# Plain PSUM copies of K and Q, zero-plane K, fixed V slots and paired 64x64 projections in a two-layer attention and token-MLP kernel

## The chip, the cores and the metric

The kernel runs on one core of a Trainium2 chip. The core has five engines with a queue of instructions each: TensorE (PE; its weight loads are listed apart as PEld), VectorE (DVE), ScalarE (ACT), GpSimd (POOL) and SyncE (SP, which here only issues DMAs). Each engine works through its own queue in order and waits on semaphores where an instruction needs the result of another engine. The metric is the device time of one execution in microseconds, lower is better. Where a number has no unit below, it is microseconds.

## What is computed

Two attention blocks and two token-mixing MLPs in turn on an activation of 2048 tokens by 512 channels, in bf16. Attention has 32 heads of 16 channels and a causal window of 256 tokens; the MLP mixes along the tokens, with 1792 hidden units.

```python
def _A_ref(x, wqkv, wo):
    B, S, D = x.shape                      # 1, 2048, 512
    H = 32; Dh = D // H; W = 256
    qkv = (x @ wqkv).reshape(B, S, 3, H, Dh).transpose(2, 0, 3, 1, 4)
    q, k, v = qkv[0], qkv[1], qkv[2]
    scores = jnp.einsum("bhqd,bhkd->bhqk", q, k) * (Dh ** -0.5)
    idx = jnp.arange(S)
    mask = (idx[:, None] - idx[None, :] >= 0) & (idx[:, None] - idx[None, :] < W)
    p = _softmax(jnp.where(mask[None, None], scores, -1e9), axis=-1)
    o = jnp.einsum("bhqk,bhkd->bhqd", p, v)
    return o.transpose(0, 2, 1, 3).reshape(B, S, D) @ wo

def _B_ref(x, w1, b1, w2, b2):
    h = _layernorm(x, axis=-1)
    u = _gelu(jnp.einsum("bsd,sf->bdf", h, w1) + b1)
    y = jnp.einsum("bdf,fs->bds", u, w2) + b2
    return y.transpose(0, 2, 1)

x = x + _A_ref(_layernorm(x), A_wqkv, A_wo)
x = x + _B_ref(_layernorm(x), B_w1, B_b1, B_w2, B_b2)
x = x + _A_ref(_layernorm(x), A_wqkv, A_wo)
x = x + _B_ref(_layernorm(x), B_w1, B_b1, B_w2, B_b2)
```

## The kernel before

**Tiling of attention.** The tokens are taken in four spans Q of 512. In each span the 512 channels are four tiles t of 128, eight heads each. For each (Q, t) there are nine steps m: step m lets each block of 32 queries meet one block of 32 keys of the window, so nine steps cover the 256 keys before a query and its own block. `bank_segments` gives the two or three stretches of queries in a step that use one key block each, and `emit_scores` (L688) makes four matmuls per stretch, in the four 64x64 quarters of the array. A quarter works on 64 channels (four heads) and yields two heads by 32 keys, so the other heads' channels must be zeroed on one side. A step is then `emit_scores` into two of the PSUM banks 0 to 3, one exp over both banks on ScalarE (`emit_exp`, L699), a multiplication of the edge of the window (L716, VectorE or GpSimd), and `emit_pv` (L737), which multiplies with V in 64x64 quarters too and accumulates in banks 4 and 5. There are 144 steps in a layer. When the ninth step is done, the two banks are copied out (`copy_out`, L360 or L362), sums of the softmax go by DMA to `den_c`, their reciprocal is spread by 64x64 matmuls (L781) and multiplied in (L788).

**Masks.** `project` (L530) makes a tile of K, Q or V: four matmuls of 128x128 by 512 tokens into bank 6 or 7. `masked` (L541 on VectorE, L546 on ScalarE) takes K and Q out of PSUM twice as wide as they are: each value times a column that is one or zero, so that K has two copies with half the heads zeroed and Q two with even or odd 16-channel groups zeroed. `job_v` copies a V tile (L360, L362), transposes it in 32x32 blocks on VectorE (L605) and spreads it beside a static pattern of ones (L590), which yields the sums of the softmax.

**The rest.** `job_outproj` (L657) multiplies by wo, adds the residual (L661) and takes statistics (L464). LayerNorm is `ln_stats` and `ln_apply`. `job_transpose` brings a normalised tile to channel-major form, by TensorE (L519) in the first span of a layer and by DMA (L511) in the others. `u_product` (L864) is the first MLP product, `job_u_part` part of it ahead of time, during the last two spans of attention; `job_u` adds the gelu (L912). `job_y` (L937) is the second product, 16 tiles of tokens; in layer 0, eight of these come before the attention of layer 1 starts and eight are put among it. Weights w1 and w2 are loaded into whatever buffers are free then (`w1_place`, `w2_place`): `w1buf`, `xhT`, `k_sb`, `q_sb`, `oU`.

**What sets the order.** Each operation is registered with `plan.op`, with the tiles that it reads and writes, and gets a number in the order of registration. `ORDER` holds, for each engine, the queue as a list of these numbers, two characters each; it is fixed in the file, and `Plan.needs` derives the semaphore waits from the dependences. The durations given to `plan.op` don't act on the order any more, only on the order of several waits of one instruction. `BANKS` says for each projection whether it goes to bank 6 or 7. SP's queue has all loads and stores, DMA transposes and the moves from `oU` and `o2`, in order.

Of the kernel before, what the change touches and what calls it, by code (L numbers as in the profile page):

```python
# [6 lines left out]
dt = mybir.dt  # L7
ALU = mybir.AluOpType
# [6 lines left out]
WARM = 10  # L15
NPARTS = (6, 6)
PARTQ = (0, 1)
UP0, UPD = 0.5, 3.3
MASKED = 1215
# [10 lines left out]
ArAsAtAuAvBGBIAwAxBKBMBQBOBUBSAyDQCbByBmClAzCgCrC0CvCZDyA0CkC6DBCuBqDHCzDLC5DADUDhDbDGDKDjBuDSDpDYDuC+B2D1D6DfDoGrECD-DtEHFXEMD0D5D+EXGPEgEGELEQEnEbEw  # L30
EsE1GhEfE6EmErE-E0FHE5FMF0FTE+FGFLFaFQFCFvF2HlF7FZFuGAFzGHF6F-GLGSHYGcGGGKGkICGoGRGVGuHKG1GjGnG8G6HBGtG0G4HFHAHNIQHVHEHeHMHaHiHSHrI1HyHdH6HhHqH-HxHuH5
IIH+INKoIcIHIMIgIkIoIVIsKWIyIfIjIrI7IxI6JAJqJWH1JbI-JjJFJaJDJnJgJvJ2JzJeJ7JmJ-KyKMJuJyJ6KQLsKZJ+KjKLLdKrKPKvMIK1KYKcK8LRLDKqKuK0K7LIK-LHLMLBLULLLTLXLa
NLLjLpNVLxNOL4LiLoMALfLwMFL3L-MEMNL0MSMMMRMgNEMoMkMZMsNzMwMjMnM0L7M8MvMzNBNjNHM7NQNTNaNANGNgMVNqNNNXNwNdN4NfN8NpOROJNvN3ONPBOWN7OIOMOhOTOaOlOqOsOkOwPp
O3OpOvO9O2NtPEPIQbO8PVM3PNPDPHPiPYPcPMPSPQPwPmNnPbPhP1PfP7PlQDPvP0PrQKP6QCQJQUO6QYQNQeRaOUQiQnQrQXQyQdQhQmQ4RCQ8QxRGP+RNQ3Q7RRQHRXRBRKRfRURkRQRWReRpRj
RoR3R2QvSxS0R6R7R8S1S3S6S2SyS9SuSJSzS4SGSvS+SMSYS7SQSUS5S-SwSrSoS8SsStSpTGSqTITCTETKTQTRTYTkTcTUTZTATdTVTlTgThTMTOUSUNUET-UTUOUAUFUyU5U6U+UuUqU-UsUoUj
U3UwUkVwVLVhVXUzVfWyVqVlVPWzVTVpVzV4YvWBYwWEV9VbYKWNWJVyV3V8W3YLWcWDWIWVWiWSWMWUWkXHWpWuWZXpXVWgW-W6Z7WoXEWtXMXWXRW5W+XlZGZxXDXuXLXzXQXeYTX8YBX4XtXyYo
YQX3YGagYAYYYFYPYXYdaKYkYcYhYrahZBZIbRZNYqZAZSZFZMZRZXa4ZbZWZiZaZfbSZ0Zsb7ZhZ4ZlZ+b8aFZzZ3aMceaRZ9aEaVbaadaIaoaQaUaaa1acalaxarbFa+awa0bXa9atbEbNbMbWbl
chbgb4cib0bfbkbtcJdscFb3cWc2cNbocAcIcbcubBcMcVcaczd+c7cgc-bIdHcyc4dLepdTc+dGdXcBdkdKdSdocQdvdWdjd5e1eBdndudyeHdCeNeUeZebeAeGeMegdOekeTeXesfCeyefeje7eK
ere-evfHgefgfQe6fYe3fde+fGfPflfXfKfcfqfkfpfxf4hBf8gEgAgIg1gMf7f-gUfTgbgHgLghiigmgTgaguiTgyggglgrg6gpg+hGftgxhKg5g9hXh7hbhFhJhngPhyhWhah2i-hjh9hriBhhiL
iIiPh1iMiWh6iAiHiahkifiOiVinixiuiZi1ieikiyi5jDhliti0jIi4iqjOjCjHjWjNjVi8jejdjhjojvjskwjyj2j-kXj7jrkHjxj1j6kGkNjRkRkMkbkpkikQkWkmkqktkfk1jajbk6k-klksk0  # L40
k5k+lNlMkDmElQlRlSmNkEmTmHmKmOmIlfmFmGlcmJmLlqmMlilumQlmmPmUmBmCmDmRmgmamVmcmemqmYmum2mym3mzm6mrmmm7mvmnmkl+l-mAmWmSminOnmnanenSnPnqnTnbnfnnnyn2n3nroG
# [13 lines left out]
AiAfAWAXAhBJAVAUBNBRBVBPAkCcBzCmChCsC1CwDzC7DCDIDMDVDcDkDqDvDZB3D7D2GsEAEIEDENEYEhESEoEcEREtE2E7FAFIFNFUFbFSFwF3F8GBGIGMGTGdGlGpGvG2G9HCHGHOHWHfHjHsHz
H7IAIJIOIdIhIpItIzI8JBJXJcJkJoJwJ0J8KAKNKRKaKkKsKwK2K9LELJLNLVLbK5LkLqLyL5MBMGMOMTMhMlMtMxM1M9NCNINRNbNhNrNxA1N5N9OKOOOXOiOmOtOxO4O+NuPJPFPWPOPjPdPUPn
PxP2P8QEQLQVQZQfQjQoQzQ5Q9RHRORSRYRgRlRqR4SkR0R+RxRzSETJTDTFTLTHTBTfTbTXTnTTTjTNTPUiUgUfVYViVmVQVrV5VUV0WCV+VKWFVJVcWOWKW4WdWWWlXIWvWqWbXqW7XAXFXNXSXm
ZHX0XvXfX9YCX5YHYRYZYeYlYsZCZJZOZTZYa5ZjZcT2ZtZ1Z5Z-aGaNaSaWapaea2aybGa-bYbObmbhb5b1cKcGcXcObpcccvc0c8dAdIdMdUdYdldpdwd6eCeIeOeVeceheleteze8eLfAfIfRfZ
fefmfrf5f9gFgJgNgVgcgigngvgzg7g-hHhLhYhchohzh3gQh+iChtiJiQiXibigioivi2izi6jEjJjPjXjfjpjtjjjzj3j8kIkOkSkckjknkuk2khk7lAlOlUjcl4mhl6mdmfmbmZmpmtmxm1m5m9
mXmlmj""",  # L60
    "gpsimd": """
AJAKASALAMANAOAgATAPA-BDB9B-CGCHCACICJAYCKAlB+AoCLAqBfCMBhCjBkBlCxBiCyC3CNC8C9DJApDDCODECPDdB6DlDOCQDWDXFnCRCSFpFsEBD9D3D4FqFrCBEZCTEJEpEKEiEjEqCUE8E9
FBE4CVEeFcFOFdFyCWF4CYF+B7GNGCGDGUHoHpGqGmGwG3G+IFGzHIHXHgIUHkCXCCH8H0B8IBIKCEJPIPJRILIqI9I+IuI0JYJTJSI5CDCFJpJdJ1JlJxJ9KEKGKtK3KxKJLKLvLOLlK6LzLrMHMi
MmMuNDM+MLNJNcNSNKNsNyNiOBN-ODOPOQOEOHOFOYOnOGO5O1PKOyPGPPPePkPyPoP3QWQaQgQFQpQ0QkQ1Q6RTRPRhRuRrRmR5RsRwSdSfSjT1UcUeVjVZTyVkVEVtTxVnVGTwVHV-WPWQWLWfWm
WnWwWYW8W9WsTzXOY5XnXoY7Y8YDY+YEYIX7X-YSY9YmYgYtYaYuYbZDZET0ZPZQYWZZZdZVaHa8aXaOaPaqa3afaDbHbPbdbjcLcHb2cncPcYcxcdc1cpc9dBdNbrcrdmdacsd7dqcqeDdredePeW
cTemeeeSe0fFe9eufBfJfnfsf6fogGdcdegWgOdigdhPhZdghRhdhUdhh4iDhpfwiSiciYiKi3idiGjKjLjQjYjuj9j4kPkTkKlEkvk3lGlJlIlPlzl1l5""",
    "sync": """
# [1004 lines left out]
```

## Time and profile before

The median of three runs is 490.74 (489.39 to 492.39). The profiled execution has a span of 487.7 from its first to its last instruction, at a TensorE clock of 1.00 throughout.

| stage | from to (us) | what runs |
|---|---|---|
| start | 0 to 12.4 | loads, LayerNorm of the first span, first projections |
| attention, layer 0 | 12.4 to 163 | 144 steps, projections, a part of the first MLP product |
| MLP, layer 0 | 163 to 222 | first product, gelu, first tiles of the second product |
| turn, then attention of layer 1 | 222 to 390 | 144 steps, with the rest of the second product among them; first exp at 228.1 |
| MLP, layer 1 | 390 to 487.7 | first and second product, stores |

| engine | busy (us) | of it |
|---|---|---|
| PE | 466.1 | scores L688 107.6, PV L737 88.8, projections L530 85.4 |
| DVE | 331.4 | masks of K and Q L541 66.8, statistics L464 43.0, edges L716 43.3 |
| ACT | 320.1 | exps L699 261.1 |
| POOL | 199.3 | edges L716 107.7, V L590 25.4 |

A group's line in the profile reads: source line, engine, operation, output and input by name, their shapes, count, then the busy time in us and the mean in ns of one, then the idle time of the engine just before them and what ended it. A line by windows gives the window, its length, and for PE, PEld, DVE, ACT and POOL the busy time and the count, then the granted clock, the share of the DMA engines and GB/s. A line of waits gives who waited for whom, the sum in us, how often, and the longest. DMA lines end with the KB of each and the median us from issue to landing.

### The profile page before, as it was taken

To read this page: it belongs to the slowest core of one execution; us is meant where nothing else is said; L and a number is where in the kernel's file an instruction comes from. 1 tells how busy PE (TensorE), PEld (TensorE's weight loads), DVE (VectorE), ACT (ScalarE), POOL (GpSimd) and SP (SyncE) were. 2 spreads that over 40 slices of the span, in tenths; PEclk is the share of its full clock that TensorE was granted. 3 is DMA by queue.
4 is the path that set the end of the run, shared out by engine and by line. 5 is a ranking of instruction groups with operands and counts; after the bars stand their busy time and mean duration, and the time that the engine had idled before them with its cause. 6 is when DMAs were issued, how large, how long until landed. Compare 5 with 4: busy or idle time off the path is not lost.

```text
span 487.7 us, 17207 instructions
## 1 busy us (share of the span) xinstructions
PE 466.1 (96%) x7608; PEld 255.6 (52%) x7706; DVE 331.4 (68%) x703; ACT 320.1 (66%) x392; POOL 199.3 (41%) x363
## 2 busy tenths in 40 slices
PE   8999989999999999999999999999999999999997
PEld 7545555565565444444445555555556544444444
DVE  7999999988885450258868588899978636120323
ACT  7999999999999203412777799999999811340000
POOL 6978878537645010001326734757363401000000
PEclk9999999999999999999999999999999999999999
DMA  6442326112145630440024300030410569013723
GB/s 195 110 98 62 28 9 150 50 29 87 50 134 169 195 87 23 140 140 12 16 46 107 99 27 5 27 91 7 132 45 8 166 184 262 1 55 108 214 87 118
DMA packets 84394, 43.59 MB, mean 89 GB/s; under 512 B 19680, under 2 KB 83296, under 8 KB 84320
## 3 DMA queue, kind: packets, MB, share of 16 engines
q1 hardware_dynamic: 80448, 42.48, 30.8%
q0 software_dynamic: 3872, 0.02, 1.3%
q8 instruction: 60, 0.98, 0.8%
q14 instruction: 14, 0.11, 0.1%
HBM read 32.51 MB, written 2.10 MB: 71 GB/s over the span
## 4 chain that ended last, share of the span: by engine, by line
PE 74%; DVE 11%; ACT 6%; DMA 4%; issue 2%; SPq 2%; ACTq 0%
PE ps L937 19%; PE ps L864 17%; PE ps L530 11%; PE ps L688 11%; PE ps L737 8%; ACT p_sb L699 6%; PE ps L657 4%; DVE k_sb L541 2%; SPq L354 2%; DVE stats L464 2%; PE ps L781 2%; DMA oU<-o 1%; DMA x_sb<-in_A_x_dram 1%; DVE oT L788 1%; DMA xhT<-in_B_w_dram 1%
## 5 line engine op out<-in xcount | busy, mean ns | idle before, releaser
L699 ACT ACTIVATE p_sb<-ps 128x1024 bf16<-128x1024 f32 (+7 forms) x288 | 261.1, 973 | 30.5 <-PE ps L688 26.7
L716 POOL TENSOR_TENSOR p_sb<-p_sb,edge 128x256 bf16<-128x256 bf16 (+2 forms) x225 | 107.7, 495 | 107.4 <-ACT p_sb L699 96.9
L688 PE MATMUL ps<-q_sb,k_sb 64*64 64x288 bf16 (+8 forms) x2816 | 107.6, 250 | 1.3 <-ACT p_sb L699 0.7
L530 PE MATMUL ps<-xhT,wqkv 128*128 128x512 bf16 x324 | 85.4, 380 | 8.3 <-issue 5.3
L737 PE MATMUL ps<-p_sb,v_all 64*64 64x288 bf16 (+8 forms) x2816 | 88.8, 246 | 1.5 <-DVE p_sb L716 0.8
L688 PEld LDWEIGHTS ps<-q_sb,k_sb 64*64 64x64 bf16 x2816 | 53.0, 106 | 55.1 <-ACT p_sb L699 33.9
L737 PEld LDWEIGHTS ps<-p_sb,v_all 64*64 64x64 bf16 x2816 | 59.4, 107 | 12.4 <-issue 4.7
L937 PE MATMUL ps<-uT,w1buf 128*128 128x512 bf16 x271 | 63.1, 379 | 1.0 <-DVE p_sb L716 0.3
L941 DVE SCALAR_TENSOR_TENSOR x_sb<-ps,b2col,x_sb 128x512 bf16<-128x512 f32 x31 | 22.3, 745 | 50.3 <-PE ps L937 50.1
L716 DVE TENSOR_TENSOR p_sb<-p_sb,edge 128x64 bf16<-128x64 bf16 (+2 forms) x175 | 43.3, 270 | 12.3 <-ACT p_sb L699 11.9
L530 PEld LDWEIGHTS ps<-xhT,wqkv 128*128 128x128 bf16 x376 | 30.3, 98 | 39.7 <-issue 4.9
L486 POOL TENSOR_TENSOR rstd<-vare,mhalf 128x4 f32<-128x4 f32 x15 | 15.3, 1023 | 78.6 <-DVE vare L484 39.4
L864 PE MATMUL ps<-xh_sb,w1buf 128*128 128x512 bf16 x178 | 43.4, 380 | 1.9 <-issue 1.4
L464 DVE BATCH_NORM_STATS2 stats<-x_sb 128x6 f32<-128x512 bf16 x64 | 43.0, 682 | 2.3 <-DMA x_sb<-in_A_x_dram 1.8
L937 PEld LDWEIGHTS ps<-uT,w1buf 128*128 128x128 bf16 x280 | 26.6, 98 | 32.4 <-issue 0.7
L541 DVE TENSOR_TENSOR k_sb<-ps,half 128x1024 bf16<-128x1024 f32 (+1 forms) x29 | 34.8, 1200 | 6.6 <-PE ps L530 5.3
L937 PE MATMUL ps<-uT,oU 128*128 128x512 bf16 x150 | 34.8, 379 | 0.2
L541 DVE TENSOR_TENSOR q_sb<-ps,even 128x1024 bf16<-128x1024 f32 x27 | 32.7, 1210 | 1.9 <-PE ps L530 1.8
L657 PE MATMUL ps<-wo_sb,oT 128*128 128x512 bf16 x116 | 30.2, 380 | 1.7 <-issue 1.1
L864 PE MATMUL ps<-xh_sb,k_sb 128*128 128x512 bf16 x124 | 30.6, 380 | 0.3 <-issue 0.2
L912 ACT ACTIVATE uT<-ps,b1col 128x512 bf16<-128x512 f32 x16 | 10.5, 682 | 30.4 <-PE ps L864 30.4
L496 ACT ACTIVATE xh_sb<-x_sb,shift,rstd 128x512 bf16<-128x512 bf16 x9 | 7.0, 805 | 34.5 <-POOL shift L490 34.5
(89 smaller groups left out, 464.4 us busy)
## 6 DMA issues: line engine op xcount, KB each, us to landing
w1buf<-in_B_w_dram SPq DMA_DIRECT2D x50, 256.0 KB, 3.5
oU<-in_B_w_dram SPq DMA_DIRECT2D x18, 256.0 KB, 5.3
oU<-o SPq DMA_DIRECT2D x16, 256.0 KB, 2.4
k_sb<-in_B_w_dram SPq DMA_DIRECT2D x16, 256.0 KB, 4.0
xhT<-in_B_w_dram SPq DMA_DIRECT2D x8, 256.0 KB, 4.2
q_sb<-in_B_w_dram SPq DMA_DIRECT2D x8, 256.0 KB
out_dram<-x_sb SPq DMA_DIRECT2D x15, 128.0 KB, 2.6
x_sb<-in_A_x_dram SPq DMA_DIRECT2D x5, 256.0 KB
```

Source lines behind the costliest of these rows:

```text
L464: dve(lambda e: e.bn_stats(stats[:, t, :], x_sb[:, t, :]), 690, prio, reads=[R("x", t)], writes=[R("stats", t)])
L486: pool(lambda e: e.tensor_tensor(rstd[:, sl], vare[:, sl], mhalf[:], op=ALU.pow), 1000, prio, reads=[R("vare", g), R("mhalf")], writes=[R( ...
L530: last = e.matmul(ps[:, b, :], lhsT=wqkv[:, c, c0:c0 + P], rhs=xhT[:, buf, c, :], start=(c == 0), stop=(c == 3))
L541: return e.tensor_tensor(dst, src.unsqueeze(2).to_broadcast([P, n, 2, w]), mask[:].unsqueeze(1).unsqueeze(3).to_broadcast([P, n, 2, w]), o ...
L657: last = e.matmul(ps[:, b, :], lhsT=oT[:, buf, t, i * P:(i + 1) * P], rhs=wo_sb[:, t, :], start=(t == 0), stop=(t == 3))
L688: last = e.matmul(ps[64 * c:64 * c + 64, 2 * half + r, 32 * i0:32 * i1], lhsT=k_sb[rows, ring, t, kb % 16, :], rhs=q_sb[rows, t, c, 32 * i ...
L699: latest[0] = plan.op({ACT: (170 + int(2 * (512 - c0) * 0.84), lambda e: e.activation(p_sb[:, slot, :, c0:512], ps[:, 2 * half:2 * half + ...
L716: return e.tensor_tensor(v, v, g, op=ALU.mult)
L737: last = e.matmul(ps[64 * r:64 * r + 64, B_O + (c ^ r), 32 * i0:32 * i1], lhsT=v_all[rows, col:col + 64], rhs=p_sb[rows, slot, r, 32 * i0: ...
L864: r = e.matmul(ps[:, b, :], lhsT=blk[:, n, (ft % 2) * P:(ft % 2 + 1) * P], rhs=xh_sb[:, 4 * g + n, :], start=(first and g == quarters[0] a ...
L937: r = e.matmul(ps[:, b, :], lhsT=blk[:, fc, (st % 2) * P:(st % 2 + 1) * P], rhs=uT[:, fc, :], start=(fc == 0), stop=(fc == NFT - 1))
L941: dve(lambda e: e.scalar_tensor_tensor(x_sb[:, st, :], ps[:, b, :], b2col[:, st:st + 1], x_sb[:, st, :], op0=ALU.add, op1=ALU.add), 750, prio,
```

## The change

**K.** The projection leaves PSUM by one plain copy into `kT` (`store_k`), and four DMAs on SP's queue carry every fourth partition each into one of four planes of `k_sb`, which are zero elsewhere. `k_sb` is now [tile, slot of eight key blocks, plane, 256] with three slots; a score's weights are 64 columns read with a step of eight elements. The planes are zeroed once at the start and again after layer 0's MLP, which uses them for w1. The first tile of layer 0 is written to its planes directly, by a multiplication with `four`.

**Q.** One plain copy (`store_q`), no masks; `q_sb` is half as large and no longer holds w1.

**Weights.** For the planes, the channels of K and Q must be permuted inside a tile, so wq and wk are loaded into `w1buf` as they are and permuted by an engine into `wqkv`, as wv was before.

**V.** Slots are [slot, block, 96] with the ones in columns 32 to 63, shared by the two halves; the spreading is four operations per tile instead of one or two.

**Pairs.** Projections of K and Q of a tile, two tiles of V, two of the output projection, two of the early first product, and two of the later second product are registered as a pair (`pair`), with two banks. Where `CELLS` has a 1 (18 of 78), both products run in 64x64 quarters, in two passes with the halves of the rows exchanged; else each runs in 128x128 as before, and the two needn't be neighbours in the queue.

**Order.** All queues, `BANKS`, the homes of w2 in layer 0 and the given durations are new; twelve tiles of the second product of layer 0, not eight, are put at or after the start of layer 1's attention. The pool of semaphores for SP's DMAs grows from 16 to 32. The sums of the softmax take two DMAs per pair of tiles instead of three, the move to `oU` two instead of one.

```diff
-        q_sb = sb("q_sb", [P, 4, 2, 512])
-        k_sb = sb("k_sb", [P, 2, 4, 16, 64])
+        q_sb = sb("q_sb", [P, 4, 512])
+        kT = sb("kT", [P, 512])
+        k_sb = sb("k_sb", [P, 4, 3, 4, 256])
...
-        for c, h in ((1, 0), (0, 0), (1, 1), (0, 1)):
-            c0 = c * D + 256 * h
-            load(wqkv[:, :, c0:c0 + 256], w_src[:, :, c0:c0 + 256], 1 << 18, -100, writes=[R("wqkv", c, h)])
+        for c, h in ((1, 0), (0, 0), (1, 1), (0, 1), (2, 0), (2, 1)):
+            load(w_natural(c, h)[0], w_src[:, :, c * D + 256 * h:c * D + 256 * h + 256], 1 << 18, -100, writes=w_natural(c, h)[1])
...
+            if c < 2:
+                turn_weights(c, h, 0, o.rearrange("p k (g v d) -> p (k g) v d", g=4, v=4), d.rearrange("p k (g d v) -> p (k g) v d", g=4, v=4), 690)
...
+        def pair(make, n, prio, reads, pieces=None):
+            a, b = misc_bank(), misc_bank()
+            pairs.append((a, b))
+            if CELLS[len(pairs) - 1] == "0":
...
+            for half in range(2):
+                for lo, hi in pieces or ((0, n),):
+                    def f(e, half=half, lo=lo, hi=hi):
+                        for k in range(lo, hi):
+                            for r in range(2):
+                                i = r ^ half
+                                rows = slice(64 * r, 64 * r + 64)
+                                lhs, rhs = make[i](k, rows)
+                                for c in range(2):
+                                    last = e.matmul(ps[64 * c:64 * c + 64, (a, b)[i], :], lhsT=lhs(c), rhs=rhs,
+                                                    start=(half == 0 and k == 0), stop=(half == 1 and k == n - 1),
+                                                    skip_group_check=True, tile_position=(64 * r, 64 * c))
...
+        def store_k(Q, t, b, prio):
+            copy_out(kT.rearrange("p (s n b) -> p s b n", s=2, b=8), ps[:, b, :].rearrange("p (s b n) -> p s b n", s=2, b=8), b, prio, 691, [R("kT")])
+            s0, s1 = k_slots(Q)
+            for v in range(4):
...
+                load(dst[:, 0:2], kT[v:P:4, :].rearrange("p (s n) -> p s n", s=2), 1 << 15, prio, reads=[R("kT")],
+                     writes=[R("k", t, n, v) for n in (s0, s1)])
+        def store_q(Q, t, b, prio):
+            copy_out(q_sb[:, t, :], ps[:, b, :], b, prio, 691, [R("q", t)])
...
                             last = e.matmul(ps[64 * c:64 * c + 64, 2 * half + r, 32 * i0:32 * i1],
-                                            lhsT=k_sb[rows, ring, t, kb % 16, :], rhs=q_sb[rows, t, c, 32 * i0:32 * i1],
+                                            lhsT=k_sb[rows, t, n].rearrange("p v n -> p (v n)")[:, 512 * c + k0:512 * c + 512:8],
+                                            rhs=q_sb[rows, t, 32 * i0:32 * i1],
...
-            for st in range(NT):
...
+            for st in range(NT if L else 4):
+                todo.append((base + 131 + st, lambda p, st=st, L=L: job_y(st, st % 6, L, p)))
+            if L == 0:
+                for s2 in range(2, NT // 2):
+                    p = BASE + (1 + 3 * (s2 - 2) if s2 < 4 else 12 + 6 * (s2 - 4) if s2 < 6 else 26 + 6 * (s2 - 6))
+                    todo.append((p, lambda p, s2=s2: job_y_pair(s2, 0, p)))
```

More of the change, by code (lines that the diff above doesn't have):

```diff
@@ L354, in load, with copy_out @@
             return plan.op({SP: (600, lambda e: e.dma_start(dst, src))}, prio=prio, dma=size, **kw)
-        def copy_out(dst, src, bank, prio, work, writes, engines=(DVE, ACT)):
+        def copy_out(dst, src, bank, prio, work, writes, engines=(DVE, ACT), held=()):
             on = {}
@@ new lines, in zero, with zero_k @@
+        def zero(dst, words, prio, writes, after=()):
+            flat = dst.bitcast(dt.float32)
+            plan.op({DVE: (60 + int(words * 1.042), lambda e: e.memset(flat, 0.0)), POOL: (110 + int(words * 0.833), lambda e: e.memset(flat, 0.0))},
+                    reads=list(after), writes=writes, prio=prio)
+        def zero_k(t, n, prio, after=()):
+            zero(k_sb[:, t, n].rearrange("p v n -> p (v n)"), 512, prio, [R("k", t, n, v) for v in range(4)], after)
+        for t in range(1, 4):
+            for n in range(2):
+                zero_k(t, n, -97)
@@ L529, in f @@
                 for c in range(4):
-                    last = e.matmul(ps[:, b, :], lhsT=wqkv[:, c, c0:c0 + P], rhs=xhT[:, buf, c, :], start=(c == 0), stop=(c == 3))
+                    last = e.matmul(ps[:, bank, 0:256], lhsT=w[:, c, :], rhs=xhT[:, 0, c, cols], start=(c == 0), stop=(c == 3))
                 return last
-            pe(f, 866, prio, reads=([R("wqkv", 2, (c0 - 2 * D) // P, r) for r in range(2)] if which == 2 else [R("wqkv", which, (c0) % D // 256)]) + [R("xhT", buf, i) for i in range(4)],
-               writes=[BK(b)])
```

552 lines of the change are left out of this document (299 added, 253 removed).

## The prediction

> **What bounds the kernel now.** I read, in this order: the page's first part, the busy time by stages, the timeline of a few microseconds, the table of groups, and the waits.
>
> ```profile
> span 487.7 us, 17207 instructions
> PE 466.1 (96%) x7608; PEld 255.6 (52%) x7706; DVE 331.4 (68%) x703; ACT 320.1 (66%) x392; POOL 199.3 (41%) x363
> ```
>
> TensorE is busy 96%, but its ends are modelled, so I work its load out again from the starts. The timeline shows a projection among attention work (start, length, then what):
>
> ```profile
> 119.22 0.39 PE L688 MATMUL ps<-q_sb,k_sb 64*64 64x288 bf16 x8
> 119.54 1.04 PE L530 MATMUL ps<-xhT,wqkv 128*128 128x512 bf16 x4
> 120.51 0.43 PE L688 MATMUL ps<-q_sb,k_sb 64*64 64x32 bf16 x12
> ```
>
> In the chain, 49 back-to-back 128*128 matmuls of the MLP take 10.74 us, the last one 0.38: (10.74 - 0.38) / 48 = 0.216 each, 512 columns at 2.4 per ns. The score step at 119.22 has two groups of four 64*64 matmuls, 288 and 224 columns; streamed at that rate they are through at 119.44, yet the projection starts at 119.54. Its four matmuls last to 120.41, yet the next score starts at 120.51. Each change between 64*64 and 128*128 work thus costs about 0.095. Reading the weight loads in order (all are recorded, some matmuls are not), the array changes 274 times: 129 in the first attention (12 to 163 us), 126 in the second (240 to 390). TensorE's load is then: 1386 matmuls of 512 columns by 0.216 = 299; narrower ones 12; the 64*64 groups 122 by their columns, and 6 for a few ns between 1536 groups; changes 274 x 0.095 = 26. Sum 465 of 487.7. The rest, 22.5, is 3.8 at the start, 3.5 at the end, 9.0 in the first attention (6.0 of it from 25 to 75) and 4.9 from 222 to 385.
>
> Busy time by stage (window, length, then each engine):
>
> ```profile
> 50.00:75.00 25.00, 22.78 (x612) 13.82 (x619) 24.04 (x45) 23.89 (x26) 20.12 (x33) 1.00 0.27 42
> 100.00:125.00 25.00, 23.96 (x619) 14.43 (x612) 22.39 (x45) 23.88 (x27) 14.92 (x25) 1.00 0.23 69
> 238.00:260.00 22.00, 21.36 (x269) 10.75 (x272) 16.33 (x36) 17.17 (x26) 9.07 (x21) 1.00 0.24 61
> ```
>
> The columns are PE, PEld, DVE, ACT, POOL. From 50 to 75 VectorE and ScalarE are both full (24.0 and 23.9 of 25) and TensorE has slack; from 100 to 125 all three are near full; from 238 to 260 only TensorE is. So attention of layer 0 is held by ScalarE and, early, VectorE; layer 1 and the MLPs by TensorE. The waits agree:
>
> ```profile
> PEld ps L688 <- ACT p_sb L699: 33.9, 83, 0.8
> ACT p_sb L699 <- PE ps L688: 26.7, 35, 7.6
> ```
>
> Scores wait for exps to free a bank 83 times, exps for scores 35 times (one of them the 7.6 us at the layer's turn).
>
> **The change, part by part.** The sum is made against this execution's 487.7 span; the median of the runs is 490.7, so 3.0 lie around the span and stay.
>
> ```profile
> L541 DVE TENSOR_TENSOR k_sb<-ps,half 128x1024 bf16<-128x1024 f32 x28 | 34.1, 1218 | 6.5 <-PE ps L530 5.3 <-PE ps L688 1.0
> L541 DVE TENSOR_TENSOR q_sb<-ps,even 128x1024 bf16<-128x1024 f32 x27 | 32.7, 1210 | 1.9 <-PE ps L530 1.8
> L360 DVE CAST vT<-ps 128x512 bf16<-128x512 f32 x20 | 13.6, 678 | 0.7 <-PE ps L530 0.6
> L362 ACT ACTIVATE vT<-ps 128x512 bf16<-128x512 f32 x12 | 7.2, 603 | 0.7 <-PE ps L530 0.6
> ```
>
> *Copies of K and Q.* Removed: 66.8 us of VectorE masks. Added: 62 plain copies. In the new queues 45 stand on vector (0.678 each: 30.5) and 17 on scalar (0.603: 10.3, against some 11 for its masks now). VectorE gains 36, ScalarE nothing.
>
> *V.* The spreading goes from 40 operations to 128 pieces of 256 outputs: 69 on vector, 55 on gpsimd, 4 on scalar. The trace has 512 outputs at 0.463 and 1024 at 0.698 on VectorE, 1.168 and 2.136 on GpSimd; by their slope 0.35 and 0.68 for 256. VectorE does 69 x 0.35 = 24 for 15 now, GpSimd 38 for 25. VectorE's net gain is 27, about 13 in each attention: 9% of a stage.
>
> *Changes of the array.* Each operation of the new tensor queue can be named from its number and its neighbours (a K,Q pair is two tensor operations, a copy, four DMAs, a copy). Eighteen of the 78 pairs are 64*64 and stand among scores. Counting changes along the new queue gives 210, 98 in the first attention and 104 in the second. 64 fewer x 0.095 = **-6.1**: -2.9 and -2.7 in the attentions. A pair in cells streams 8 x 512 columns either way, so nothing else is lost or won.
>
> *Slack.* With VectorE 9% lighter, banks 6 and 7 come free sooner (0.68 for 1.22 after a projection). Of the 13.9 idle TensorE has from 12 to 163 and from 222 to 385, I take back 5 (0 to 10; the middle, as I know no row that divides it): **-5**. A cap: in layer 0 ScalarE is busy 142 of 148 us and its work stays, so that layer can't gain over 5.9. My share for it, -2.9 - 3.2 = -6.1, would need it never to wait; I take -4.2: **+1.9**.
>
> *The start.* wq and wk are now loaded whole and turned by an engine before the first projection: by the 128x1024 row of ScalarE at L433, 1.05, part of it behind LayerNorm; the first K goes to four planes (1.22 for 0.69, two halves). Before, the first exp is at 12.42. **+1.5** (0 to 3). The zero fills and the y tiles moved into layer 1 cost nothing: GpSimd is 41% busy, and the y work is the same matmuls, where TensorE was full anyway. If that cover is gone, 22 fills by the 0.95 of `spread`'s memset are 21 us of GpSimd.
>
> *K by DMA.* 31 tiles x 4 = 124 DMAs join SP's queue.
>
> ```profile
> oU<-o SPq DMA_DIRECT2D x16, 256.0 KB, 2.4
> ```
>
> SP needs 0.57 to 0.65 to issue such a DMA (den_c rows), so K is there after 0.68 + 4 x 0.6 + about 2.4 = 5.5. Behind a waiting K DMA on SP stand den_c, the transposes of xh (1.24 each to issue) and w1. From the new tensor queue, TensorE work between a K product and the first score that needs it is 4.8 and 5.0 us at the first tile of spans 0 and 2 of layer 1, 6.2 at the next shortest, 6.5 to 25 elsewhere. Two tiles are late by 0.6 each, some by more where another DMA is between: **+1.5** (0 to 16, rival C).
>
> *Strided K.* A score's weights are now 64 columns that lie 16 bytes apart. No row has such a load. The trace bounds the contiguous one: a group of 32 columns (13 ns of streaming) is followed by the next after 28 ns, so four 64x64 loads fit in 28. Between no slower (0) and four times (112 ns) I take twice, since most segments (288 columns, 122 ns) hide even four: it then shows behind segments of 32, 64 and 96 columns, 28 + 28 + 14 in nine steps, by 32 turns = 2.2, half on the binding stage: **+1.0** (0 to 12). [...]
>
> Sum: -6.1 - 5 + 1.9 + 1.5 + 1.5 + 1.0 = -5.2; 490.7 - 5.2 = **485**.
>
> **The rivals.** A, the forecast: 480 to 488, **chance 0.45**.
>
> B, the whole slack goes: -6.1 and -10, layer 0 reaching its cap, start +1: 476 (474 to 480). For it: VectorE is at 96% where TensorE has its slack. Against: ScalarE keeps 130 us of exps per layer. **0.15**.
>
> C, K comes late: the DMA takes the place of the mask as what scores wait for. If SP and the 16 rings are occupied by other transfers (loads land after 3.5 to 5.3 in the page), the way takes 8.5 instead of 5.5; against the leads read from the queue ten tiles are then late by 0.1 to 3.7, together 16, and TensorE, in order, stands: 490.7 - 5.2 - 1.5 + 16 = 500. It outweighs the gain from a way of about 7 us (2.2 + 2.0 + 0.8 + 0.5 = 5.5). Against it: DMA engines are 20 to 40% busy in these stages. **0.13**.
>
> D, strided loads at four times: 84, 84, 70, 56, 43, 30, 16 and 3 ns beyond the segments of nine steps, 386 x 32 = 12.4, minus the 1.0 counted: 497. **0.08**. [...]
>
> E, it doesn't do what it says: ScalarE is the bound in both attentions, its queue grows from 378 to 389 operations, and each change of the array saved only lengthens TensorE's wait for an exp: start and K eat the rest, 490.5 (488.5 to 493). **0.19**.
>
> **How the numbers follow.** The likeliest is A: 485; its own range is 480 to 488. A measurement of this kernel tells no change from 0.5%, that is 488.3 to 493.2. Faster: A and B, 0.60. Same: E, 0.19. Slower: C and D, 0.21. For 8 in 10 the range leaves out the best of B and the most of C and D: 475 to 496.
>
> **What would show it.** The changes read from weight loads fall from 274 to about 210, each still 0.095. VectorE's busy time falls by 20 to 30, ScalarE's stays within 5. The first exp is at 13 to 15. In the waits, scores wait for a K DMA a few times only; C shows as a wait on that DMA over 5 us. D shows as groups of 32 and 64 columns in scores followed only after 50 ns or more, while such groups of the PV matmuls, whose weights lie together, keep 28. I am wrong if the attentions are not 1 to 5 us shorter each, or if the time after is in the MLP stages, which the change leaves alone.

## Result and profile after: slower, by 16%

The kernel with the change takes 567.89 us (median, 562.99 to 570.25) beside 490.31 (489.39 to 492.39) for the kernel before in the same runs: ratio 1.157, 95% interval 1.151 to 1.164. I had forecast 485, range 475 to 496.

The first part of the page and the busy time by stage (window, length, then PE, PEld, DVE, ACT, POOL, each with its count, then the granted clock); the third window begins 10 us after layer 1's first exp, as 238 to 260 did before:

```profile
span 567.5 us, 18509 instructions
PE 500.2 (88%) x8106; PEld 304.8 (54%) x8186; DVE 360.9 (64%) x772; ACT 345.9 (61%) x400; POOL 207.4 (37%) x380
...
50.00:75.00 25.00, 20.14 (x380) 12.76 (x384) 22.02 (x49) 16.66 (x21) 15.23 (x31) 0.86 0.34 82
100.00:125.00 25.00, 20.89 (x510) 14.98 (x503) 24.08 (x49) 19.52 (x21) 11.32 (x18) 1.00 0.30 52
281.00:303.00 22.00, 18.62 (x321) 10.97 (x317) 15.98 (x40) 14.49 (x20) 12.33 (x27) 1.00 0.16 41
```

VectorE was to lose 20 to 30 us of work and has 29.5 more. ScalarE, which was full in layer 0 (23.9 of 25), now runs 16.7 and 19.5 of 25 and stands idle for the rest: the bound has moved to what feeds it. The groups that the change added or touched:

```profile
L756 PE MATMUL ps<-q_sb,k_sb 64*64 64x288 bf16 (+8 forms) x2816 | 133.1, 289 | 15.8 <-ACT p_sb L768 5.3 <-DVE k_sb L639 3.6 <-DMA k_sb<-kT 3.1
L756 PEld LDWEIGHTS ps<-q_sb,k_sb 64*64 64x64 bf16 x2816 | 107.2, 202 | 60.7 <-ACT p_sb L768 23.9 <-issue 20.6 <-ACT q_sb L382 6.4
L805 PEld LDWEIGHTS ps<-p_sb,v_all 64*64 64x64 bf16 x2816 | 61.1, 110 | 15.6 <-DVE p_sb L785 4.4 <-issue 3.0 <-POOL p_sb L785 2.3
L380 DVE CAST kT<-ps 128x512 bf16<-128x512 f32 x22 | 54.0, 2455 | 7.8 <-PE ps L560 3.3 <-DMA k_sb<-kT 2.4 <-issue 2.0
L382 ACT ACTIVATE kT<-ps 128x512 bf16<-128x512 f32 x9 | 22.2, 2471 | 0.5 <-DMA k_sb<-kT 0.3 <-PE ps L560 0.2
L380 DVE CAST q_sb<-ps 128x512 bf16<-128x512 f32 x23 | 16.0, 695 | 5.0 <-PE ps L574 2.9 <-PE ps L560 2.1
```

Two rows stand out. The copy of K has the shape, the types and the source of the copy of Q, yet it takes 2.46 us where Q's takes 0.70: it writes its 2-byte elements 16 bytes apart. And the weight loads of the scores (L756), which read 64 columns that lie 16 bytes apart, take 202 ns, while those of the PV matmuls (L805), with columns side by side, take 110. Here is what a copy of K does to the others, in order of time (start, length, engine and line, idle time before and who ended it):

```profile
65.38 1.94 ACT L768 ACTIVATE p_sb<-ps 128x1024 bf16<-128x1024 f32 x2 [0.16 <-PE ps L756]
...
66.95 2.42 DVE L380 CAST kT<-ps 128x512 bf16<-128x512 f32 x1 [0.73 <-issue]
...
69.43 1.92 PE L574 MATMUL ps<-xhT,wqkv 64*64 64x512 bf16 x16 [3.36 <-DVE kT L380]
...
71.13 0.64 PE L756 MATMUL ps<-q_sb,k_sb 64*64 64x256 bf16 x8
...
71.83 1.02 ACT L768 ACTIVATE p_sb<-ps 128x1024 bf16<-128x1024 f32 x1 [4.51 <-PE ps L756]
```

VectorE copies K out of a bank from 66.95 to 69.37. TensorE's next pair needs that bank and waits 3.4 us; the scores stand behind the pair in TensorE's queue; ScalarE has no scores and waits 4.5 us. After the wait the 16 matmuls of the pair take 1.92 us, though the same 16 take 1.06 in both_straight (below). The wait and what follows it in the change, by windows, then that pair in both_straight:

```profile
66.00:69.40 3.40, 0.07 (x4) 0.00 (x0) 2.67 (x3) 1.31 (x2) 1.20 (x3) 0.79 0.01 2
69.40:74.80 5.40, 5.37 (x80) 3.34 (x84) 3.22 (x8) 2.05 (x2) 2.74 (x6) 0.50 0.31 74
...
60.78 1.06 PE L574 MATMUL ps<-xhT,wqkv 64*64 64x512 bf16 x16
```

The granted clock is 0.50 in the 5.4 us after the wait (1.00 in both_straight from 50 to 75, and in the change itself from 409.9, where 16 such matmuls take 1.06): TensorE came out of the wait at half its clock. By half microseconds it is 1.00 up to 67.5 and 0.50 from 68.0, so it fell some 1.9 us into the wait. In this trace it fell three more times, at 16.8, 88.5 and 423.0, in or just behind waits of TensorE of 3.59, 1.55 and 2.15 us; waits of 1.90 and 2.12 us, up to 409.9 and 458.9, came without a fall, so what sets it is not shown. ScalarE's waits for scores in all (us, times, longest):

```profile
ACT p_sb L768 <- PE ps L756: 69.5, 93, 4.5
```

Before, exps waited 26.7 us for scores.

Where the time went, read from the 288 exps (us: start of the first; from there to the end of layer 0's last; from there to the start of layer 1's first; from there to the end of layer 1's last; the rest of the span):

| kernel | first exp | layer 0 | turn | layer 1 | rest |
|---|---|---|---|---|---|
| before | 12.4 | 144.3 | 71.4 | 163.4 | 96.2 |
| after | 19.2 | 179.0 | 73.0 | 199.2 | 97.1 |
| copy_straight | 18.2 | 163.0 | 73.5 | 176.3 | 97.3 |
| weights_straight | 18.9 | 174.2 | 73.2 | 191.8 | 97.5 |
| both_straight | 18.1 | 156.4 | 72.8 | 168.8 | 97.5 |
| both_start_nopairs | 15.5 | 156.0 | 73.9 | 171.1 | 97.4 |
| both_edgelight | 14.6 | 152.9 | 73.9 | 169.1 | 97.2 |
| k_two_apart_light | 14.5 | 149.0 | 74.0 | 170.5 | 97.2 |

Of the 79.8 us between the two spans, 34.7 are in the attention of layer 0, 35.8 in that of layer 1 and 6.8 at the start. The MLP stages are as before.

### The profile page after: what moved, and what is told of

The parts are those of the page before. It is cut to its first block, busy times and chain, and to the rows that moved or that the text cites. A ratio compares the mean times of both kernels' runs of the same rounds, so it can differ in the third digit from the quotient of the medians.

```text
span 567.5 us, 18509 instructions
## 1 busy us (share of the span) xinstructions
PE 500.2 (88%) x8106; PEld 304.8 (54%) x8186; DVE 360.9 (64%) x772; ACT 345.9 (61%) x400; POOL 207.4 (37%) x380
## 3 DMA queue, kind: packets, MB, share of 16 engines
q8 instruction: 64, 1.05, 0.8%
## 4 chain that ended last, share of the span: by engine, by line
PE 59%; DVE 18%; ACT 7%; DMA 5%; issue 5%; SPq 4%; POOL 1%; DVEq 0%; ACTq 0%; POOLq 0%
PE ps L560 16%; PE ps L930 11%; PE ps L756 10%; PE ps L1021 9%; DVE kT L380 7%; PE ps L805 6%; SPq L374 4%; PE ps L574 4%; DMA k_sb<-kT 4%; ACT kT L382 3%; ACT p_sb L768 3%; DVE p_sb L785 2%; PE ps L849 1%; PE ps L475 1%; DVE v_all L658 1%
## 5 line engine op out<-in xcount | busy, mean ns | idle before, releaser
L768 ACT ACTIVATE p_sb<-ps 128x1024 bf16<-128x1024 f32 (+8 forms) x288 | 268.2, 980 | 72.1 <-PE ps L756 69.5
L785 POOL TENSOR_TENSOR p_sb<-p_sb,edge 128x256 bf16<-128x256 bf16 (+2 forms) x200 | 96.2, 489 | 161.8 <-ACT p_sb L768 121.5
L756 PE MATMUL ps<-q_sb,k_sb 64*64 64x288 bf16 (+8 forms) x2816 | 133.1, 289 | 15.8 <-ACT p_sb L768 5.3
L756 PEld LDWEIGHTS ps<-q_sb,k_sb 64*64 64x64 bf16 x2816 | 107.2, 202 | 60.7 <-ACT p_sb L768 23.9
L805 PE MATMUL ps<-p_sb,v_all 64*64 64x288 bf16 (+8 forms) x2816 | 91.1, 249 | 4.3 <-DVE p_sb L785 2.5
L560 PE MATMUL ps<-xhT,wqkv 128*128 128x512 bf16 x237 | 63.9, 392 | 16.5 <-DVE p_sb L785 3.6
L805 PEld LDWEIGHTS ps<-p_sb,v_all 64*64 64x64 bf16 x2816 | 61.1, 110 | 15.6 <-DVE p_sb L785 4.4
L380 DVE CAST kT<-ps 128x512 bf16<-128x512 f32 x22 | 54.0, 2455 | 7.8 <-PE ps L560 3.3
L658 POOL TENSOR_TENSOR v_all<-vB,evens 128x256 bf16<-128x256 bf16 x55 | 37.7, 689 | 29.0 <-DVE vB L676 28.9
L560 PE MATMUL ps<-uT,w1buf 128*128 128x512 bf16 x156 | 38.3, 380 | 2.8 <-issue 1.1
L574 PE MATMUL ps<-xhT,wqkv 64*64 64x512 bf16 x416 | 28.9, 398 | 7.6 <-DVE kT L380 4.8
L1021 PE MATMUL ps<-uT,oU 128*128 128x512 bf16 x151 | 34.7, 379 | 0.4 <-issue 0.2
L856 DVE TENSOR_TENSOR oT<-oU,ps 128x512 bf16<-128x512 f32 x32 | 21.3, 688 | 16.9 <-PE ps L849 16.7
L930 PEld LDWEIGHTS ps<-xh_sb,k_sb 128*128 128x128 bf16 x192 | 18.1, 98 | 22.4 <-DMA k_sb<-in_B_w_dram 0.7
L728 DVE TENSOR_TENSOR x_sb<-x_sb,ps 128x512 bf16<-128x512 bf16 x32 | 21.7, 683 | 11.5 <-PE ps L560 8.9
```

What stands on the lines that cost most here:

```text
L380: on[DVE] = (work, lambda e: e.tensor_copy(dst, src))
L560: last = e.matmul(ps[:, bank, :], lhsT=lhs(None), rhs=rhs, start=(k == 0), stop=(k == n - 1))
L574: last = e.matmul(ps[64 * c:64 * c + 64, (a, b)[i], :], lhsT=lhs(c), rhs=rhs, start=(half == 0 and k == 0), stop=(half == 1 and k == n - 1 ...
L658: return e.tensor_tensor(d, src.unsqueeze(2).to_broadcast([P, 8, 2, DH]), evens.rearrange("p (h d) -> p h d", h=2).unsqueeze(1).to_broadca ...
L756: last = e.matmul(ps[64 * c:64 * c + 64, 2 * half + r, 32 * i0:32 * i1], lhsT=k_sb[rows, t, n].rearrange("p v n -> p (v n)")[:, 512 * c + ...
L768: latest[0] = plan.op({ACT: (180 + int(2 * (512 - c0) * 0.832), lambda e: e.activation(p_sb[:, slot, :, c0:512], ps[:, 2 * half:2 * half + ...
```

## The experiments

My theory after the result: accesses in steps of 16 bytes cost the time (K's copy by its writes, the scores by their weights). The rival: K's way through the DMA queue, the new queues and the pairs themselves. All ratios are to the kernel before, measured beside each group of runs.

| kernel | median us | ratio | 95% interval |
|---|---|---|---|
| after | 567.9 | 1.157 | 1.151 to 1.164 |
| copy_straight | 529.3 | 1.080 | 1.074 to 1.087 |
| copy_turned | 527.4 | 1.079 | 1.076 to 1.082 |
| weights_straight | 556.8 | 1.139 | 1.136 to 1.142 |
| both_straight | 515.8 | 1.055 | 1.052 to 1.058 |
| k_blocks | 536.4 | 1.095 | 1.091 to 1.100 |
| k_blocks_start | 534.8 | 1.091 | 1.087 to 1.096 |
| k_blocks_nopairs | 531.4 | 1.086 | 1.080 to 1.091 |
| v_light | 533.0 | 1.088 | 1.081 to 1.095 |
| both_start | 517.0 | 1.053 | 1.047 to 1.059 |
| both_start_nopairs | 514.8 | 1.046 | 1.040 to 1.052 |
| k_apart | 515.9 | 1.050 | 1.043 to 1.058 |
| turned_start_nopairs | 530.1 | 1.078 | 1.073 to 1.084 |
| both_vlight | 514.0 | 1.050 | 1.041 to 1.060 |
| both_edgelight | 510.0 | 1.040 | 1.037 to 1.044 |
| both_velight | 516.9 | 1.056 | 1.050 to 1.062 |
| before_edgelight | 487.3 | 0.995 | 0.993 to 0.996 |
| k_two | 512.6 | 1.047 | 1.042 to 1.053 |
| k_two_apart_light | 506.6 | 1.034 | 1.030 to 1.039 |

### The two stepped accesses, alone and together

copy_straight:

```diff
-copy_out(kT.rearrange("p (s n b) -> p s b n", s=2, b=8), ps[:, b, :].rearrange("p (s b n) -> p s b n", s=2, b=8), b, ...
+copy_out(kT[:], ps[:, b, :], b, ...
```

> K leaves PSUM as a copy in order; its keys then lie in another order in the planes, so the scores are those of other keys, with the same work. Theory 1 (2-byte elements written 16 bytes apart are what costs): the copy falls from 2.46 to 0.68 us on VectorE and from 2.47 to 0.60 on ScalarE, 22 x 1.78 + 9 x 1.87 = 56 us of engine time, most of it on engines that are full in the attentions; time 520 to 535. Rival (K's way by DMA and the new queues are what costs, the copy only fills a wait): scores then wait for the K DMA instead, and the time stays over 555.

weights_straight:

```diff
-lhsT=k_sb[rows, t, n].rearrange("p v n -> p (v n)")[:, 512 * c + k0:512 * c + 512:8],
+lhsT=k_sb[rows, t, n].rearrange("p v n -> p (v n)")[:, 512 * c + 64 * k0:512 * c + 64 * k0 + 64],
```

> The scores take 64 weight columns that lie together in place of 64 that lie 16 bytes apart (other keys, same work); the copy of K stays as it is. Theory 1: the loads fall from 202 to about 107 ns, a group of 32 columns is followed after 28 ns again, and TensorE loses some 25 us of load; since the copies of K still hold the banks, 10 to 25 of it shows: 543 to 558. Rival (the strided load is hidden by the streaming, the longer spacing has another cause): the spacing stays and the time is within 3 us of 568.

both_straight has both edits:

> Both edits at once (other keys, same work). Theory 1: the two costs are nearly all that the change lost after the start, so the time is 490 to 505: the 490 of before, plus 7 for the longer start, minus up to 6 for fewer changes of the array. Rival (queues, pairs or K's way by DMA cost too): over 515, with a wait in the trace that is neither a copy of K nor a load of K.

copy_turned keeps layout and keys, and moves the step from the write to the read:

```diff
-copy_out(kT.rearrange("p (s n b) -> p s b n", s=2, b=8), ps[:, b, :].rearrange("p (s b n) -> p s b n", s=2, b=8), b, ...
+copy_out(kT.rearrange("p (s n b) -> p s n b", s=2, b=8), ps[:, b, :].rearrange("p (s b n) -> p s n b", s=2, b=8), b, ...
```

> K ends where it did, with the same keys, but the copy writes in order and reads PSUM 128 bytes apart instead. Theory 1a (only the stepped write is slow): 0.68 us a copy and the time of copy_straight, 520 to 535. Theory 1b (any step of 16 bytes or more is slow, on either side): still about 2.4 us a copy and 560 to 570.

Measured: 529.3, 556.8, 515.8 and 527.4. The group of K's copy in copy_straight, then in copy_turned:

```profile
L380 DVE CAST kT<-ps 128x512 bf16<-128x512 f32 x22 | 15.1, 687 | 8.0 <-PE ps L560 3.8 <-DMA k_sb<-kT 2.9 <-PE ps L756 1.2
```

```profile
L380 DVE CAST kT<-ps 128x512 bf16<-128x512 f32 x22 | 15.1, 685 | 5.8 <-PE ps L560 2.8 <-DMA k_sb<-kT 2.7
```

The write in steps is the whole of it: 2.46 goes to 0.69 whether the read of PSUM is in order or jumps 128 bytes from element to element. The copy alone is worth 38.6 us, and copy_turned, which keeps the keys in their places, gains about as much. The weight loads, in weights_straight:

```profile
L756 PEld LDWEIGHTS ps<-q_sb,k_sb 64*64 64x64 bf16 x2816 | 58.0, 108 | 65.9 <-ACT p_sb L768 33.5 <-issue 14.0 <-ACT q_sb L382 6.3
```

From 202 to 108 ns each. From start to start, at full clock and by the median, a score group of 288 columns followed by one of 32 takes 122 ns again, where the change has 159; followed by one of 160, 126 for 212. One of 32 followed by 288 takes 28 to 53, as in the kernel before, for a median of 116. The edit alone is worth 11.1 us, the low end of what I expected, and 13.5 on top of the straight copy (529.3 to 515.8). The two add up: 49.7 apart, 52.1 together. Theory 1 holds for 52 of the 78 us. It does not hold as the whole story: both_straight missed my 490 to 505 by over 10 us, and the rival's limit (over 515) was just reached. About 26 us are left.

### Right keys with both in order

k_blocks lays the planes out in blocks of 32 keys, so that a DMA must write runs of 64 bytes (core of the edit; where two slots do not follow one another it needs two DMAs):

```diff
-k_sb = sb("k_sb", [P, 4, 3, 4, 256])
+k_sb = sb("k_sb", [P, 4, 2, 3, 512])
...
+dst = k_sb[v:P:4, t, v // 2].rearrange("p s (b w n) -> p s b w n", w=2, n=32)[:, :, :, v % 2]
...
+lhsT=k_sb[rows, t, c, n, 64 * k0:64 * k0 + 64],
```

> The planes are laid out in blocks of keys, so that K's copy is in order and a score's 64 weight columns lie together with the right keys; the DMA to the planes then writes runs of 64 bytes instead of 512, and one span in four needs 8 DMAs for 4. Theory 1 (only the two stepped accesses, of which both_straight left 516): 511 to 516, the first K being written in order too. Rival (short runs make K late): scores wait for the K DMA, over 10 us together, and the time is over 522.

k_blocks_start also turns wq and wk in order (`"p k (g v d) -> p (k g) d v"` on both sides):

> As k_blocks, and the turn of wq and wk writes in order and reads 128 bytes apart. Theory 1: the turns fall from 1.3 to 2.5 us to about 0.7 to 1.1, the first exp comes 2 to 4 us earlier than in k_blocks, and the time is as much lower: 508 to 513. Rival (the start is held by the loads of wq and wk, not by the turns): the first exp moves by less than 1 us.

k_blocks_nopairs sets all of CELLS to 0:

> As k_blocks_start, with all pairs in 128x128 again, in the same queues. Theory of the prediction (a change of the array costs 0.095 us, and TensorE sets the time): some 64 more changes, 6 us more than k_blocks_start. Rival (in these queues TensorE waits for VectorE and ScalarE, so that changes of the array are hidden): within 2 us of it. A third way: a pair in 64x64 holds both banks until its second half, so without it banks come free earlier and the time falls.

v_light:

```diff
+few = 1 if len(pieces_done) < 64 else 8
-d = v_sb[:, t, n, :, 64 * r:64 * r + 32].rearrange("p b (h d) -> p b h d", h=2)
+d = v_sb[:, t, n, 0:few, 64 * r:64 * r + 32].rearrange("p b (h d) -> p b h d", h=2)
```

> As k_blocks_start, but in layer 0 each of the 64 pieces of V writes an eighth of its outputs (the rest of V stays zero there, cleared once at the start, some 7 us of VectorE); layer 1 is complete. It takes about 10 us from VectorE and 15 from GpSimd in layer 0. Theory 2 (what is left of the loss lies in VectorE, which V's pieces and the edge masks fill again): from the first exp to the last of layer 0, 156.4 us in both_straight and 144.3 before, comes down by 6 to 10. Rival (the order of the queues, whatever VectorE has to do): down by less than 3.

Measured: 536.4, 534.8, 531.4, 533.0. This layout costs more than the contiguous weights bring. The packets of the hardware queue in both_straight, then in k_blocks, whose waits follow (us, times, longest):

```profile
q1 hardware_dynamic: 91152, 46.55, 34.0%
```

```profile
q1 hardware_dynamic: 147216, 46.56, 38.3%
```

```profile
DVE kT L380 <- DMA k_sb<-kT: 11.3, 7, 2.7
PE ps L770 <- DMA k_sb<-kT: 6.7, 2, 3.6
```

For the same bytes there are 56,000 more packets, in 156 DMAs of K for 124, and now VectorE and the scores (L770 there) wait 18.0 us for K's DMAs, as rival C of the prediction had it; no run parts the short runs from the 32 added DMAs. both_straight has one such wait of note:

```profile
DVE kT L380 <- DMA k_sb<-kT: 2.4, 3, 2.1
```

So C was a real danger, but for DMAs worse than those of the change. The first exp moved only from 15.1 to 14.6 in k_blocks_start, less than expected: there the turns were not what held the start. In v_light layer 0 takes 165.5 us for 171.5 in k_blocks_start, 6.0 less, the low edge of theory 2. But clearing V at the start puts its first exp at 20.9 for 14.6, and layer 0 ends at 186.4 us for 186.1. The run does not bear theory 2 out. Leaving the pairs out gained 3.4 instead of losing 6, though the two intervals overlap.

### The start, the pairs, K's DMAs

both_start is both_straight with the start in order as well, both_start_nopairs that without 64x64 pairs, k_apart that with K's DMAs to a place of their own, and turned_start_nopairs the version with the keys in their places:

> As both_straight (other keys, same work), and the start written in order too: the turn of wq and wk, and the first K to its planes. In both_straight the first exp came at 18.1, in k_blocks_start, where the start was mended in the same way, at 14.6. Theory 1: the first exp is at 14 to 15 and the time 3 to 4.5 below the 515.8 of both_straight. Rival (layer 0 gives the gain back, since VectorE is full there whatever comes first): the first exp moves, the time by less than 1.5.

> As both_start, with all pairs in 128x128. In k_blocks the 18 pairs in 64x64 cost 3.4 us, where I had put them at a gain of 6.1. Theory 3 (a 64x64 pair holds two banks until its second half is through, and what stands behind waits for both copies): 2 to 5 us below both_start. Rival (the prediction: fewer changes of the array; in k_blocks it was the late K that made pairs dear): 3 to 6 above it.

```diff
-dst = k_sb[v:P:4, t, s0::s1 - s0, v, :] if s1 > s0 else k_sb[v:P:4, t, s0::s1 - s0, v, :]
+dst = k_off[v:P:4, :, v, :]
...
-writes=[R("k", t, n, v) for n in (s0, s1)])
+writes=[R("k_off", v)])
```

> As both_start_nopairs, but the DMAs of K write to a place of their own and the scores read the planes as they stand (zeros, after the first tile), so that no score waits for a DMA of K; every operation is still issued and takes as long. Theory C (K's way by DMA is what is left over): 8 us or more below both_start_nopairs. Rival (DMAs of K are in time, as the 1.3 us that scores wait for them in both_straight says): within 3.

> The right keys: copy_turned (527.4) with the start in order (as in both_start, the first K by a turned read) and no pairs in 64x64; the strided weights stay. If the gains add: 3.5 for the start and 3.4 for the pairs, 519 to 522. If the strided weights make TensorE the bound, fewer changes of the array are worth more there and leaving the pairs out gains nothing: 523 to 527.

Measured: 517.0, 514.8, 515.9, 530.1. The first K's write to four planes, after, then in both_start:

```profile
L639 DVE TENSOR_TENSOR k_sb<-ps,four 128x1024 bf16<-128x1024 f32 x1 | 4.7, 4708 | 0.3 <-PE ps L628 0.3
```

```profile
L639 DVE TENSOR_TENSOR k_sb<-ps,four 128x1024 bf16<-128x1024 f32 x1 | 1.2, 1225 | 0.3 <-PE ps L628 0.3
```

The same operation in order takes a quarter, and the first exp comes at 14.7 instead of 18.1. Yet the time doesn't fall (517.0 beside 515.8): the rival held. In the traces layer 0 gives the 3.4 us back (160.3 for 156.4); layer 1 is 3.9 longer too, in an execution 3 us above the median. The pairs are worth -2.2 (theory 3, but with overlapping intervals I only take from it that they don't gain 6). Theory C falls: 515.9 beside 514.8. The last kernel gains nothing over copy_turned (530.1 beside 527.4) and missed both of its ranges; the gains do not add, and why is open.

### What is left: VectorE's load, or the order

both_vlight, both_edgelight and both_velight take load off both_start_nopairs; before_edgelight is the control.

```diff
-def f(e, c=c, ec=ec, w=w, k=k):
+def f(e, c=c, ec=ec, w=8, k=k):
```

> As both_start_nopairs, but in layer 0 each of the 64 pieces of V writes an eighth of its outputs (the rest of V is cleared once at the start, 7 us of VectorE). Layer 0 lasts 156.0 us there from its first exp to its last, 144.3 before. Theory V (VectorE and GpSimd have too much to do in layer 0): 145 to 151. Theory O (the order of the queues): above 153.

> As both_start_nopairs, but each edge mask covers 8 columns instead of 32 to 256, in both layers, which takes some 35 us from VectorE and 60 from GpSimd, half of it in layer 0. Theory V: layer 0 falls from 156.0 to about the 144.3 of before or below it, and the time by 12 or more. Theory O: layer 0 stays above 151, and the time falls by less than 7.

> Both reliefs together. Theory V: layer 0 at 144 or below, where ScalarE's 142 us of work end it. Theory O: still 149 or more, with VectorE well under full in layer 0.

> The kernel before with edge masks of 8 columns, the same relief as in both_edgelight. ScalarE is busy 142 of the 144 us of layer 0 there, so I expect at most 3 us in all: 487 to 491. If it falls by 8 or more, VectorE held the kernel before as well, and both_edgelight's gain says nothing about what the change lost.

Layer 0 lasts 149.3, 152.9 and 155.1 us, against 156.0 without relief; the times are 514.0, 510.0 and 516.9. The 149.3 lies in theory V's range, but there too the clearing of V delays the first exp, to 20.8 for 15.5: layer 0 ends at 170.1 us, for 171.5 without relief, and with both reliefs at 175.9. So only both_edgelight is a clean test. I had put the relief by narrow masks too high: VectorE's masks fall from 60.4 to 38.1 us, not by 35. In layer 0 VectorE has 14.6 us less to do (118.8 for 133.4), and layer 0 is 3.1 shorter. VectorE's load by itself is therefore not it. From 62.5 to 75 us, in the first half of layer 0, before, then in both_edgelight:

```profile
62.50:75.00 12.50, 11.12 (x296) 6.68 (x294) 11.67 (x20) 11.47 (x13) 9.41 (x18) 1.00 0.41 57
```

```profile
62.50:75.00 12.50, 10.24 (x296) 6.19 (x288) 8.97 (x20) 9.57 (x11) 7.01 (x17) 1.00 0.84 73
```

VectorE has 2.7 us less to do and is far from full, and still TensorE and ScalarE do less than before. The same stretch of both_edgelight in order of time shows one reason; the last line gives the landing times of K's DMAs (min, median, max):

```profile
66.94 0.61 SPq L374 DMA_DIRECT2D k_sb<-kT  x1
...
71.90 0.69 DVE L380 CAST kT<-ps 128x512 bf16<-128x512 f32 x1 [2.36 <-issue]
...
72.65 0.64 PE L849 MATMUL ps<-rc,spread 64*64 64x128 bf16 x32 [1.93 <-DVE kT L380]
...
74.23 1.02 ACT L768 ACTIVATE p_sb<-ps 128x1024 bf16<-128x1024 f32 x1 [2.01 <-PE ps L756]
...
DMA to landing us min/median/max: 1.8/2.0/4.9
```

The DMA issued at 66.94 reads the copy of K before, out of the one buffer kT, and is the one that took 4.9 us to land, at 71.82. The next copy of K starts at 71.90, and TensorE and ScalarE stand behind it for 2 us each. So VectorE can hold the others while it is idle. The control loses 2.7 us, as expected.

k_two gives K's copies two buffers kT in turn, and k_two_apart_light takes away most of what was suspected (V's spreading stays):

```diff
-kT = sb("kT", [P, 512])
+kT2 = sb("kT2", [P, 2, 512])
...
+one = len(k_turn) % 2
+kT = kT2[:, one]
```

> As both_start_nopairs (514.8), with two buffers kT in turn, so that a copy of K doesn't wait for the DMAs that read the one before it. Theory K (the single buffer strings copy, four DMAs and the next copy together, and TensorE waits for the bank): 505 to 510, layer 0 at 150 or less. Rival (VectorE waits 2.4 us in all for these DMAs, as the waits of both_straight say): within 3.

> As k_two, and K's DMAs write to a place of their own (no score waits for them) and the edge masks cover 8 columns. If the suspected waits were hiding one another: 495 or less, layer 0 near the 144.3 of before. Theory O (the order in which each engine takes its work): 503 to 510, layer 0 at 150 or more.

Measured: 512.6 and 506.6. Two buffers are within 3 us (the rival). With all that off, the time is in theory O's range and layer 0, at 149.0, a little under its 150 (144.3 before); layer 1 takes 170.5 (163.4), with VectorE at most 19.1 of 25. Some 17 us are left, 11.8 of them in the two attentions, and what was taken away doesn't hold them. All these kernels share the new queues, so the order in which each queue takes its work is the likeliest cause; but they share the finer spreading of V too, no run changes the order alone, and it stays open. No version came near the kernel before.

## Why the prediction was wrong

**Copies of K and Q: the step that failed.** I priced "62 plain copies" by the rows of vT, 0.678 and 0.603. For Q that was right (0.695 and 0.598). For K it was not: the copy is plain in its arithmetic, not in its addresses, and takes 2.455 and 2.471. That is 22 x 1.78 + 9 x 1.87 = 56 us of engine time that the sum lacked; taking it away gives 38.6 us of time. The diff shows the cause: `kT.rearrange("p (s n b) -> p s b n")` has n as its innermost index, with a step of 8 elements. I saw that step where the weights read it, and not where the copy writes it.

**Strided K: direction right, hiding wrong.** I allowed from no slower to four times, took twice, and said that segments of 288 columns hide even four. One load does take twice as long (202 for 106 ns), but it isn't hidden: such a segment is followed after 159 to 212 ns instead of 122 to 126. The term of +1.0 (12 at most) measured 11.1 alone and 13.5 with the copy mended. That rival D priced it at 12.4 is in part luck, as D let those long segments hide their loads. The sign that I had named for D was there (32 columns followed after 116, PV at a median of 29), though its limit of 50 was too low: in the kernel before, half of these groups already took 52. The factor of two was my estimate, and no row of before had such a load. The runs show the cost of the step for these loads (202 ns, 108 with the columns side by side) and for K's writes (2.46 us, 0.69 in order), and none for a copy's read of PSUM at 128 bytes apart (0.685 us, 0.687 in order).

**Slack and VectorE's relief: did not come.** Even with the copy mended, VectorE has 331.9 us of work in both_straight, for 331.4 before. K, Q and V went as I had worked out (in layer 0 by the trace's records: 31.5 of masks out, 16.9 of copies in, V 7.8 to 13.2). I missed the edge masks: the new queues move some from GpSimd to VectorE. Before, then in both_start_nopairs, VectorE's share:

```profile
L716 DVE TENSOR_TENSOR p_sb<-p_sb,edge 128x256 bf16<-128x256 bf16 x57 | 18.8, 339 | 5.3 <-ACT p_sb L699 5.0
L716 DVE TENSOR_TENSOR p_sb<-p_sb,edge 128x128 bf16<-128x128 bf16 x61 | 14.6, 248 | 1.7 <-ACT p_sb L699 1.6
L716 DVE TENSOR_TENSOR p_sb<-p_sb,edge 128x64 bf16<-128x64 bf16 x57 | 12.3, 223 | 5.3 <-ACT p_sb L699 5.2
```

```profile
L785 DVE TENSOR_TENSOR p_sb<-p_sb,edge 128x256 bf16<-128x256 bf16 x68 | 25.5, 380 | 10.0 <-ACT p_sb L768 10.0
L785 DVE TENSOR_TENSOR p_sb<-p_sb,edge 128x64 bf16<-128x64 bf16 x71 | 18.2, 260 | 6.0 <-ACT p_sb L768 4.9 <-POOL p_sb L785 0.6
L785 DVE TENSOR_TENSOR p_sb<-p_sb,edge 128x128 bf16<-128x128 bf16 x61 | 16.7, 279 | 6.7 <-ACT p_sb L768 6.6
```

Their sum is 45.7 us before and 60.4 here (43.3 and 58.7 with overlapping records counted once), 25 masks more and each slower, for a reason that no run shows. So the -5 rested on a relief that isn't there, and both_edgelight says that it would have brought little anyway: 14.6 us off VectorE in layer 0 took 3.1 off the layer. The idle time from which I took the 5 was also not fully placed: its parts add up to 21.2 of the 22.5.

**Changes of the array.** 208 counted for 210 predicted, but the -6.1 that hung on them is not in the time: without the pairs there are 284, and the time is 2 to 3 us lower, with overlapping intervals. I had counted what a change costs TensorE and not that a pair in 64x64 fills both banks until its end; that this is what eats the gain is argued, not shown. (The split had a slip that the sum didn't use: 126 less 104 is 22 changes, 2.1 us and not 2.7.)

**The start.** +1.5 was mis-sized, for the same reason as the copy: the first exp is 6.8 later. The turns of wq and wk write in steps of 8 bytes and take 2.43 us on GpSimd, 2.50 on ScalarE and 1.30 on VectorE, for the 1.05 that I took. But with the copy and the weights mended, a start 3.4 us earlier was worth nothing, as layer 0 made up for it.

**K by DMA.** Right: 0.60 to issue, 1.9 to land, few waits (scores three times, 4.4 us together; k_apart: no gain). Rival C did not happen. Nor did E, which had ScalarE as the bound in both attentions: it waits 69.5 us for scores.

## What to carry to other kernels

Price a new operation by a row with the same step in its innermost index, on the write side above all; shape, type and engine alone were off by 3.6 times here (2.46 us for 0.68). If a transposition has to happen in a copy out of PSUM, let the read jump and the write run, as in copy_turned (0.685 us a copy, for 2.455). And when a removed cost gives back less than its size, test the relief of each suspect alone and together, and with a control, and see that the relief itself doesn't delay the start: here neither the fuller VectorE, the late start nor the pairs held what was left.

## What was not expected of the hardware

In these runs the writes with the longer step took longer, and not alike on all engines. ScalarE took 2.44 ns per 2-byte element at 8 bytes apart (2.50 us for 1024) and 4.83 at 16 bytes (2.47 us for 512); VectorE 1.27 (1.30 us) and 4.80 (2.46 us). The sources differ, SBUF for the 8 bytes and PSUM for the 16, so these are four points and no rule. GpSimd's 2.43 us at 8 bytes is close to ScalarE's. Reading PSUM 128 bytes apart cost a VectorE copy nothing (0.685 for 0.687). The turns with the step on the read side (32 bytes apart in SBUF) took 1.95 us on GpSimd and 1.99 on ScalarE, where the row that I had priced them by (ScalarE, L433 before) took 1.05. And DMA writes in runs of 64 bytes instead of 512, with 32 more DMAs and no more bytes, came with 20.6 us (536.4 for 515.8).
